# Attention units handled two at a time, with scores four units ahead and PSUM shared 4-2-2

## The chip, the core and the metric

The kernel runs on one core of one Trainium2 chip, as a single launch. The metric is the device time of that launch in microseconds (us). Five engines work side by side, each on its own stream of instructions in order: TensorE (PE; its weight loads have rows of their own, PEld), VectorE (DVE), ScalarE (ACT), GpSimd (POOL), and SyncE (SP), which here only issues DMAs. TensorE writes its results to PSUM, which holds eight banks of 128 partitions x 512 fp32; VectorE and ScalarE read them from there.

## The reference, cut to what matters

Attention with 32 global and 512 local positions per head (8 batches, 8 heads, head size 64), then a mixture of experts over all tokens:

```python
s_g = scale * q_g @ k_all.T            # global rows see everything
out_g = sm(s_g) @ v_all
s_ll = where(abs(i - j) <= 32, scale * q_l @ k_l.T, -1e9)   # a band of 32
s_l = concat([scale * q_l @ k_g.T, s_ll])                   # plus the global keys
out_l = sm(s_l) @ concat([v_g, v_l])
x = concat([out_g, out_l]) as (4352, 512)
logits = x @ w_gate                    # greedy: best (token, expert) pairs first, 544 tokens an expert
out[mask_e] = relu(x[mask_e] @ w1[e]) @ w2[e]
```

## The kernel before, in words

It has three stages in time: attention (with the gate's logits taken along), the routing, and eight experts. Only attention is touched by the change.

Attention works on **units**. A batch has ten: eight local units (`Local`, two heads by 256 rows each; two units share a pair of heads, that is one load of q, k and v) and two global units (`Glob`, four heads each). In the first seven batches the order is four local, one global, four local, one global; in the last it is two local, both global, six local. Each unit has four steps:

- `a`: scores on TensorE (L134; L195 for a global unit) into the PSUM tile `S`; a global unit takes two `S` tiles.
- `e`: mask, maximum and its negation on VectorE (L141, L143; L201 to L203), then the exponentials on ScalarE (L145; L210 to L216), into `p` (or `pg`).
- `c`: transposes of the exponentials on TensorE into the PSUM tile `T` (L150; L224, two tiles), and the copy `evac` from there into `pt` (or `pgt`).
- `d`: outputs on TensorE into the PSUM tile `O` (L162; L234), then the division on VectorE (L165 to L170; L237 to L241) into `xs` (or `xg`), which go to DRAM by DMA (L173, L243).

The gate's logits of a finished batch come as six extra steps, put between the units of the next batch: four `gate_x` (L259: transposes of one quarter of `xs` into `T`, copied by `evac` into `xt`; in the last batch into `S`), `gate_m` (L265: a product with the gate's weights into `O`, copied into `ltc`), and `gate_l` (L274: transposes into `T`, and a reduction on VectorE, L275, into `L`). The list `GS = (0, 2, 4, 6, 8, 9)` says in which units of the next batch they fall. The same steps for the global rows (`gx`) follow after the fourth and the eighth batch.

`evac` sends three of five copies to ScalarE (L251) and two to VectorE (L253). The order of the work is written out by hand: the loop below issues instructions, each engine runs its own in that order, and a tile with n buffers makes its n+1st writer wait for the first one's last reader. Every PSUM tile here is one bank: `S` 3, `T` 3, `O` 2.

```python
for i in range(-LA, nu + 3):              # LA = 2
    if i + LA < nu:
        ...                               # loads of later pairs
        units[i + LA].a()
    if 0 <= i < nu:
        units[i].c()
    if i + LA < nu:
        units[i + LA].e()
    if 1 <= i <= nu:
        units[i - 1].d()
    for f in extra.get(i, []):
        f()
```

`load_qk` brings q and k by DMA, and GpSimd spreads q into `qz` (L86); `load_v` brings v into `vw`. They are issued ahead, as the loop comes to a unit.

Of the kernel before, what the change touches and what calls it, by code (L numbers as in the profile page):

```python
# [8 lines left out]
F32 = mybir.dt.float32  # L9
# [9 lines left out]
B, H, SL, SG, D = 8, 8, 512, 32, 64  # L19
S = SL + SG  # L20
DM = H * D
# [4 lines left out]
NB = SL // 128  # L26
NW = SL // 32
# [37 lines left out]
def attention(ctx, tc, A, consts, xd, ident, L, nbatch, rt=None):  # L65
    nc = tc.nc
    ac = ctx.enter_context(tc.tile_pool(name="ac", bufs=1))
    ld = ctx.enter_context(tc.tile_pool(name="ld", bufs=3))
# [18 lines left out]
        return spread  # L87

    def load_v(b, p):
        t = ld.tile([128, 2, NW, D + 1], F32, name="vw", bufs=6)  # L90
        nc.sync.dma_start(t.rearrange("p h w d -> p (h w d)"), A["vw"][b, p])
        vw[b, p] = t

    qz = [ac.tile([128, QW // 32, 2, 32], F32, name=f"qz{i}") for i in range(NZ)]
    pg = [ac.tile([128, 6, 128], F32, name=f"pg{i}") for i in range(2)]
    mask = ac.tile([128, 2 * NB, 128], F32, name="mask")
    wg = ac.tile([128, 4, 32], F32, name="wg")
    P = [(b, p) for b in range(nbatch) for p in range(NP)]

    warm = ac.tile([128, 128], F32, name="warm")  # L100
    nc.vector.memset(warm, 0.0)
    wt = ps.tile([128, NB, 128], F32, name="T", bufs=3)
    for _ in range(WARM):
        nc.tensor.matmul(wt[:, 0, :], warm, warm, start=True, stop=True)
    for i in range(NZ):
        nc.gpsimd.memset(qz[i][64:128, :, 0, :], 0.0)
        nc.gpsimd.memset(qz[i][0:64, :, 1, :], 0.0)
    for i in range(2):
        nc.gpsimd.memset(pg[i], 0.0)
    load_qk(0, 0)(nc.vector)  # L110
    nc.sync.dma_start(mask.rearrange("p a b -> p (a b)"), A["mask"])
# [7 lines left out]
    class Local:  # L119
# [3 lines left out]
        def a(s):  # L123
            b, q = s.b, s.q
            z = qz[(b * NP + q) % NZ]
            kw = qk[b, q]
            st = ps.tile([128, NB, 128], F32, name="S", bufs=3)
            s.p = wk.tile([128, NB, 128], F32, name="p", bufs=4)
            s.nm = wk.tile([128, NB], F32, name="nm", bufs=4)
            for c in range(NB):  # L130
                for r in range(2):
                    j = 8 * s.u + 2 * c + r
                    k0 = 32 * ((3 * j + 1) // 2)
                    nc.tensor.matmul(st[64 * r:64 * r + 64, c, :], z[:, j].rearrange("p h i -> p (h i)"),  # L134
                                     kw[:, k0:k0 + 128], start=True, stop=True)
            s.st = st
# [8 lines left out]
                nc.scalar.activation(s.p[:, c, :], s.p[:, c, :], AF.Exp, bias=nm[:, c:c + 1], scale=SCALE)  # L145

        def c(s):
            t = ps.tile([128, NB, 128], F32, name="T", bufs=3)
            for c in range(NB):
                nc.tensor.transpose(t[:, c, :], s.p[:, c, :], ident)  # L150
            s.pt = wk.tile([128, NB, 128], F32, name="pt", bufs=3)
            evac(s.pt, t)
# [22 lines left out]
    class Glob:  # L175
# [2 lines left out]

        def a(s):
            b, g = s.b, s.g  # L180
            s.sa = ps.tile([128, 512], F32, name="S", bufs=3)
            s.sb = ps.tile([128, 32], F32, name="S", bufs=3)
            for part in range(2):
                for r in range(2):
                    i = 2 * g + r
                    t = qk[b, i]
                    z = qz[(b * NP + i) % NZ][:, NW].rearrange("p h i -> p (h i)")
                    if part == 0:
                        base = t[:, 64:128]
                        mv = ap_of(base, 0, [list(base.ap[0]), [96, 8], [1, 64]])  # L190
                        dd = s.sa[64 * r:64 * r + 64].rearrange("p (a b) -> p a b", b=64)
                    else:
                        mv = t[:, 32:64]
                        dd = s.sb[64 * r:64 * r + 64]
                    nc.tensor.matmul(dd, z, mv, start=True, stop=True)  # L195

        def e(s):
            b, g = s.b, s.g
            m = wk.tile([128, 8], F32, name="gm", bufs=2)
            s.m = m  # L200
            nc.vector.tensor_reduce(m[:, 0:1], s.sa, axis=AX.X, op=ALU.max)  # L201
            nc.vector.tensor_reduce(m[:, 1:2], s.sb, axis=AX.X, op=ALU.max)
            nc.vector.tensor_scalar(m[:, 2:3], m[:, 0:1], m[:, 1:2], -SCALE, op0=ALU.max, op1=ALU.mult)  # L203
            pgt = pg[(b * 2 + g) % 2]
            s.p = pgt
            f = pgt.rearrange("p a b -> p (a b)")
            d0 = f[:, 0:64]
            d1 = f[:, 512:576]
            pd = list(d0.ap[0])
            nc.scalar.activation(ap_of(d0, 0, [pd, [256, 2], [96, 3], [1, 64]]),  # L210
                                 s.sa[:, 0:384].rearrange("p (a b c) -> p a b c", a=2, c=64), AF.Exp,
                                 bias=m[:, 2:3], scale=SCALE, accum_out=m[:, 3:4])
            nc.scalar.activation(ap_of(d1, 0, [pd, [192, 2], [1, 64]]),
                                 s.sa[:, 384:512].rearrange("p (b c) -> p b c", c=64), AF.Exp,
                                 bias=m[:, 2:3], scale=SCALE, accum_out=m[:, 4:5])
            nc.scalar.activation(f[:, 672:704], s.sb, AF.Exp,  # L216
                                 bias=m[:, 2:3], scale=SCALE, accum_out=m[:, 5:6])

        def c(s):
            s.pt = wk.tile([128, 6, 128], F32, name="pgt", bufs=2)  # L220
            for lo, n in ((0, 4), (4, 2)):
                t = ps.tile([128, NB, 128], F32, name="T", bufs=3)
                for k in range(n):
                    nc.tensor.transpose(t[:, k, :], s.p[:, lo + k, :], ident)  # L224
                evac(s.pt[:, lo:lo + n], t[:, :n])
# [27 lines left out]
            nc.vector.tensor_copy(dst, src)  # L253

    def gate_x(src, xt, c, spare):
        t = ps.tile([128, NB, 128], F32, name="S" if spare else "T", bufs=3)
        n = src.shape[1]
        for k in range(n):
            nc.tensor.transpose(t[:, k, :], src[:, k, c * 128:(c + 1) * 128], ident)  # L259
        evac(xt[:, c, :n * 128], t[:, :n].rearrange("p a b -> p (a b)"))  # L260

    def gate_m(xt, n):
        lt = ps.tile([128, 512], F32, name="O", bufs=2)
        for c in range(4):
            nc.tensor.matmul(lt[32 * c:32 * c + 32, :n * 128], wg[:, c, :], xt[:, c, :n * 128],  # L265
                             start=True, stop=True)
        ltc = wk.tile([128, 512], F32, name="ltc", bufs=2)
        evac(ltc[:, :n * 128], lt[:, :n * 128])
        return ltc

    def gate_l(ltc, J, n):
        t = ps.tile([128, NB, 4, 32], F32, name="T", bufs=3)
        for k in range(n):
            nc.tensor.transpose(t[:, k].rearrange("p a b -> p (a b)"), ltc[:, k * 128:(k + 1) * 128], ident)  # L274
        nc.vector.tensor_reduce(L[:, J:J + n, :], t[:, :n, :, 0:8].rearrange("p k c e -> p k e c"),  # L275
                                axis=AX.X, op=ALU.add)

    def gate_units(b, src, J, n):
        xt = []

        def go(c):
            if c == 0:
                xt.append(wk.tile([128, 4, 128 * n], F32, name=f"xt{n}", bufs=2))
            if c < 4:
                gate_x(src(), xt[0], c, b == nbatch - 1)
            elif c == 4:
                xt.append(gate_m(xt[0], n))
            else:
                gate_l(xt[1], J, n)
        return [lambda c=c: go(c) for c in range(6)]  # L290
# [1 line left out]
    gsrc = {}  # L292

    def load_gx(i):
        t = wk.tile([128, 1, DM], F32, name="gx", bufs=2)
        for k in range(4):
            nc.sync.dma_start(t[32 * k:32 * k + 32, 0, :], xd[(4 * i + k) * S:(4 * i + k) * S + SG, :])
        gsrc[i] = t

    units = []  # L300
# [29 lines left out]
    def pairidx(u):  # L330
        if isinstance(u, Local):
            return u.b * NP + u.q
        return u.b * NP + 2 * u.g + 1

    nu = len(units)
    first = rt.setup(slice(0, 28)) if rt else None
    LA = 2
    for i in range(-LA, nu + 3):
        if rt and i == 2:
            rt.load()  # L340
        if rt and i == 12:
            rt.prepare()
        if i + LA < nu:
            while nl[0] < len(P) and nl[0] <= pairidx(units[i + LA]) + 4:
                load_qk(*P[nl[0]])(nc.gpsimd)
                load_v(*P[nl[0] - 1])
                nl[0] += 1
                if nl[0] == len(P):
                    load_v(*P[-1])
            units[i + LA].a()  # L350
        if 0 <= i < nu:
            units[i].c()
        if i + LA < nu:
            units[i + LA].e()
            if i + LA == 0:
                spread1(nc.vector)
        if 1 <= i <= nu:
            units[i - 1].d()
        for f in extra.get(i, []):
            f()  # L360
        if rt and i >= nu - 3:
            for _ in range(6):
                next(first, None)


WARM = 10
# [637 lines left out]
```

## Time and profile before

| what | value |
|---|---|
| median of 3 runs | 756.08 us (755.35 to 756.97) |
| the profiled execution | 756.55 us, span of its instructions 754.5 us |
| mean granted TensorE clock | 0.964 |
| PE busy | 697.2 us (92% of the span) |
| DVE busy | 504.8 us (67%) |
| ACT busy | 313.8 us (42%) |
| POOL busy | 159.7 us (21%) |
| data moved by DMA | 120.51 MB, mean 160 GB/s |

The profile's page gives the span in 40 slices of about 19 us, a digit for the busy tenths of each. A row of a window gives its bounds and length, then for PE, PEld, DVE, ACT and POOL the busy time and the number of instructions, then the granted clock, the DMA engines' busy share and GB/s. A row of the timeline gives the start, the length, the engine, the line, the operation, output tile<-input tiles, shapes, the count, and in brackets how long the engine was idle before it and what ended that. TensorE's own ends are modelled; the starts of its weight loads show best when a group could begin.

### The profile page before, as it was taken

The page shows a single profiled execution, that of the slowest core. Times are in us where ns is not written, and L with a number is a line of the kernel's source. Part 1 is how long each engine was busy: PE and PEld are TensorE (multiplying, and loading weights), DVE is VectorE, ACT ScalarE, POOL GpSimd, SP SyncE. Part 2 cuts the span into 40 slices and gives each one's busy share as a digit, 9 for nine tenths or more (in the row PEclk, how much of TensorE's full clock was granted, in tenths as well). Part 3 has the DMA queues.
Part 4 walks back from the last instruction along what each step waited for, and adds up shares of the span by engine and source line. Part 5 has one row for each costly group of instructions (what it writes and reads, how often), then busy time and mean ns, then how long its engine had stood idle before and what let it go on. Part 6 is the DMA issues. An engine that isn't in the chain of part 4 may idle for free. (4 is left out here: it accounts for less than half of the span.)

```text
span 754.5 us, 21122 instructions
## 1 busy us (share of the span) xinstructions
PE 697.2 (92%) x8636; PEld 560.2 (74%) x8636; DVE 504.8 (67%) x1848; ACT 313.8 (42%) x849; POOL 159.7 (21%) x190
## 2 busy tenths in 40 slices
PE   7989999999995189999999999999999999899993
PEld 6767777777673179768779878877877878888972
DVE  5887878877777778767767777766776774441300
ACT  3656665665651034234143244234333333443310
POOL 5222112221100130241241241141132043312011
PEclk9999999999998569999999999999999999999997
DMA  9997879969701160360161161261072065231000
GB/s 359 405 364 286 323 280 332 338 244 333 289 22 58 45 238 1 111 204 29 70 234 40 62 240 43 71 212 62 8 260 78 1 254 186 75 126 46 1 33 28
DMA packets 32416, 120.51 MB, mean 160 GB/s; under 512 B 6720, under 2 KB 6976, under 8 KB 24128
## 3 DMA queue, kind: packets, MB, share of 16 engines
q1 hardware_dynamic: 22080, 67.78, 24.1%
q0 software_dynamic: 10240, 51.39, 19.4%
q8 instruction: 68, 1.11, 0.6%
q14 instruction: 28, 0.23, 0.1%
HBM read 101.32 MB, written 17.83 MB: 158 GB/s over the span
## 5 line engine op out<-in xcount | busy, mean ns | idle before, releaser
L860 PE MATMUL H<-xh,w1h 128*128 128x272 f32 x512 | 153.0, 299 | 3.6 <-DVE hl L405 3.0
L860 PE MATMUL H<-xl,w1h 128*128 128x272 f32 x512 | 151.4, 296 | 0.0
L860 PE MATMUL H<-xh,w1l 128*128 128x272 f32 x512 | 151.4, 296 | 0.0
L145 ACT ACTIVATE p<-p,nm 128x128 f32<-128x128 f32 x256 | 82.1, 394 | 65.1 <-DVE ls L165 33.1
L862 ACT ACTIVATE hh<-H 128x272 fp32r<-128x272 f32 x128 | 51.0, 399 | 135.3 <-PE H L860 129.8
L888 PE MATMUL Y<-w2h,hh 128*128 128x512 f32 x256 | 103.9, 406 | 0.0
L860 PEld LDWEIGHTS H<-xh,w1h 128*128 128x128 f32 x512 | 98.0, 191 | 7.0 <-DVE hl L405 2.7
L888 PE MATMUL Y<-w2l,hh 128*128 128x512 f32 x256 | 102.8, 401 | 0.0
L888 PE MATMUL Y<-w2h,hl 128*128 128x512 f32 x256 | 102.4, 400 | 0.0
L860 PEld LDWEIGHTS H<-xl,w1h 128*128 128x128 f32 x512 | 97.9, 191 | 0.6
L860 PEld LDWEIGHTS H<-xh,w1l 128*128 128x128 f32 x512 | 97.8, 191 | 0.3
L134 PE MATMUL S<-qk,qz 128*64 128x128 f32 x1024 | 71.2, 281 | 5.5 <-DVE qz L86 2.9
L405 DVE SCALAR_TENSOR_TENSOR hl<-H,hh 128x272 fp32r<-128x272 f32 x128 | 54.6, 435 | 26.5 <-ACT h L864 12.6
L86 POOL COPY qz<-q 64x544 f32<-64x544 f32 x60 | 38.3, 639 | 149.6 <-DMA q<-in_qk_dram 109.6
L134 PEld LDWEIGHTS S<-qk,qz 128*64 128x64 f32 x1024 | 55.5, 138 | 18.3 <-issue 11.0
L742 POOL DMA_INDIRECT out_dram<-y,idx x40 | 39.7, 992 | 137.9 <-ACT y L833 84.7
L405 DVE TENSOR_TENSOR w2l<-w2r,w2h 128x512 fp32r<-128x512 f32 x64 | 43.2, 688 | 37.6 <-ACT w2h L712 37.2
L696 POOL DMA_INDIRECT w1r<-in_w_dram,widx x16 | 15.7, 979 | 229.8 <-DVE r_a L405 127.2
L141 DVE CUSTOM_DVE_ANT_0 p<-S,mask 128x128 f32<-128x128 f32 x256 | 58.7, 286 | 6.1 <-PE S L134 5.6
L833 ACT ACTIVATE y<-Y 128x512 f32<-128x512 f32 (+1 forms) x40 | 23.2, 595 | 92.8 <-PE Y L888 59.4
L888 PEld LDWEIGHTS Y<-w2h,hh 128*128 128x128 f32 x256 | 48.2, 188 | 15.8 <-issue 5.9
L712 ACT ACTIVATE w1h<-w1r 128x512 fp32r<-128x512 f32 x64 | 36.5, 624 | 49.7 <-DVE L L405 29.8
(168 smaller groups left out, 1200.7 us busy)
## 6 DMA issues: line engine op xcount, KB each, us to landing
vw<-in_vw_dram SPq DMA_DIRECT2D x32, 1040.0 KB, 7.8
qk<-in_qk_dram SPq DMA_DIRECT2D x32, 432.0 KB, 5.4
q<-in_qk_dram SPq DMA_DIRECT2D x32, 272.0 KB, 5.8
xd<-xs SPq DMA_DIRECT2D x8, 1024.0 KB, 6.8
xd<-xg SPq DMA_DIRECT2D x64, 8.0 KB, 5.3
xg<-xd,idx POOLq DMA_INDIRECT x40
out_dram<-y,idx POOLq DMA_INDIRECT x40
mask<-in_mask_dram SPq DMA_DIRECT2D x1, 512.0 KB, 4.5
```

What stands on the lines that cost most here:

```text
L86: eng.tensor_copy(z[r, :, h, :], q[r].rearrange("p (j i) -> p j i", i=32))
L134: nc.tensor.matmul(st[64 * r:64 * r + 64, c, :], z[:, j].rearrange("p h i -> p (h i)"), kw[:, k0:k0 + 128], start=True, stop=True)
L141: nc.vector.tensor_tensor_reduce(s.p[:, c, :], st[:, c, :], mask[:, 4 * s.u + c, :], 1.0, -BIG, ALU.add, ALU.max, nm[:, c:c + 1])
L145: nc.scalar.activation(s.p[:, c, :], s.p[:, c, :], AF.Exp, bias=nm[:, c:c + 1], scale=SCALE)
L405: return op(*args, **kw)
L696: nc.gpsimd.indirect_dma_start(out=dst, out_offset=None, in_=src, element_offset=off, in_offset=bass.IndirectOffsetOnAxis(ap=idx, axis=0))
L712: nc.scalar.activation(hi, raw, AF.Copy)
L742: nc.gpsimd.indirect_dma_start(out=out, out_offset=bass.IndirectOffsetOnAxis(ap=rt.idx[ph][:n, t:t + 1], axis=0), in_=y[:n], in_offset=None)
L833: nc.scalar.activation(y[:n], p[:n], AF.Copy)
L860: nc.tensor.matmul(p, w[d][:, fs], x[:, d, q], start=(d + k == 0), stop=(d + k == 5))
L862: nc.scalar.activation(hh[:, f, q], p, AF.Relu)
L888: nc.tensor.matmul(p, h[:, f, q], w[f], start=(f + k == 0), stop=(f + k == 9))
```

## The change

Attention's loop takes two units per pass. In each pass come the transposes and copies (`c`) of both, the scores (`a`) of two units four ahead, their reductions and exponentials (`e`), the outputs (`d`) of the two units just transposed, and then the extra steps of two units. `LA` goes from 2 to 4. PSUM is shared anew: `S` 4, `T` 2, `O` 2. Work buffers grow (`p`, `nm`, `gm`, `pg`, `vw`) and others shrink to one (`ltc`, `xt`, `gx`). The loads move behind `c`.

```diff
-    pg = [ac.tile([128, 6, 128], F32, name=f"pg{i}") for i in range(2)]
+    pg = [ac.tile([128, 6, 128], F32, name=f"pg{i}") for i in range(3)]
...
-            st = ps.tile([128, NB, 128], F32, name="S", bufs=3)
-            s.p = wk.tile([128, NB, 128], F32, name="p", bufs=4)
-            s.nm = wk.tile([128, NB], F32, name="nm", bufs=4)
+            st = ps.tile([128, NB, 128], F32, name="S", bufs=4)
+            s.p = wk.tile([128, NB, 128], F32, name="p", bufs=6)
+            s.nm = wk.tile([128, NB], F32, name="nm", bufs=8)
...
-            t = ps.tile([128, NB, 128], F32, name="T", bufs=3)
+            t = ps.tile([128, NB, 128], F32, name="T", bufs=2)
...
-        t = ps.tile([128, NB, 128], F32, name="S" if spare else "T", bufs=3)
+        t = ps.tile([128, NB, 128], F32, name="S" if spare else "T", bufs=4 if spare else 2)
...
-        ltc = wk.tile([128, 512], F32, name="ltc", bufs=2)
+        ltc = wk.tile([128, 512], F32, name="ltc", bufs=1)
...
-                xt.append(wk.tile([128, 4, 128 * n], F32, name=f"xt{n}", bufs=2))
+                xt.append(wk.tile([128, 4, 128 * n], F32, name=f"xt{n}", bufs=1))
...
-    LA = 2
-    for i in range(-LA, nu + 3):
+    LA = 4
+    for i in range(-LA, nu + 2, 2):
+        now = (i, i + 1)
...
+        for k in now:
+            if 0 <= k < nu:
+                units[k].c()
+        for k in now:
+            if k + LA < nu:
+                ...
+                units[k + LA].a()
+        for k in now:
+            if k + LA < nu:
+                units[k + LA].e()
...
+        for k in now:
+            if 0 <= k < nu:
+                units[k].d()
+        for k in now:
+            for f in extra.get(k + 1, []):
+                f()
```

The vw tile goes from 6 to 7 buffers, gm from 2 to 4, gx from 2 to 1.

More of the change, by code (lines that the diff above doesn't have):

```diff
@@ L89, in load_v @@
     def load_v(b, p):
-        t = ld.tile([128, 2, NW, D + 1], F32, name="vw", bufs=6)
+        t = ld.tile([128, 2, NW, D + 1], F32, name="vw", bufs=7)
         nc.sync.dma_start(t.rearrange("p h w d -> p (h w d)"), A["vw"][b, p])
@@ L101, in attention @@
     nc.vector.memset(warm, 0.0)
-    wt = ps.tile([128, NB, 128], F32, name="T", bufs=3)
+    wt = ps.tile([128, NB, 128], F32, name="T", bufs=2)
     for _ in range(WARM):
@@ L107, in attention @@
         nc.gpsimd.memset(qz[i][0:64, :, 1, :], 0.0)
-    for i in range(2):
+    for i in range(3):
         nc.gpsimd.memset(pg[i], 0.0)
@@ L180, in a @@
             b, g = s.b, s.g
-            s.sa = ps.tile([128, 512], F32, name="S", bufs=3)
-            s.sb = ps.tile([128, 32], F32, name="S", bufs=3)
+            s.sa = ps.tile([128, 512], F32, name="S", bufs=4)
+            s.sb = ps.tile([128, 32], F32, name="S", bufs=4)
             for part in range(2):
@@ L198, in e @@
             b, g = s.b, s.g
-            m = wk.tile([128, 8], F32, name="gm", bufs=2)
+            m = wk.tile([128, 8], F32, name="gm", bufs=4)
             s.m = m
@@ L203, in e @@
             nc.vector.tensor_scalar(m[:, 2:3], m[:, 0:1], m[:, 1:2], -SCALE, op0=ALU.max, op1=ALU.mult)
-            pgt = pg[(b * 2 + g) % 2]
+            pgt = pg[(b * 2 + g) % 3]
             s.p = pgt
@@ L221, in c @@
             for lo, n in ((0, 4), (4, 2)):
-                t = ps.tile([128, NB, 128], F32, name="T", bufs=3)
+                t = ps.tile([128, NB, 128], F32, name="T", bufs=2)
                 for k in range(n):
@@ L271, in gate_l @@
     def gate_l(ltc, J, n):
-        t = ps.tile([128, NB, 4, 32], F32, name="T", bufs=3)
+        t = ps.tile([128, NB, 4, 32], F32, name="T", bufs=2)
         for k in range(n):
@@ L294, in load_gx @@
     def load_gx(i):
-        t = wk.tile([128, 1, DM], F32, name="gx", bufs=2)
+        t = wk.tile([128, 1, DM], F32, name="gx", bufs=1)
         for k in range(4):
@@ L342, in attention @@
             rt.prepare()
[L343 to L363, printed above, removed]
+        for k in now:
[3 more added lines that the diff above has]
+            if k + LA < nu:
+                while nl[0] < len(P) and nl[0] <= pairidx(units[k + LA]) + 4:
+                    load_qk(*P[nl[0]])(nc.gpsimd)
+                    load_v(*P[nl[0] - 1])
+                    nl[0] += 1
+                    if nl[0] == len(P):
+                        load_v(*P[-1])
+                units[k + LA].a()
+        for k in now:
+            if k + LA < nu:
+                units[k + LA].e()
+                if k + LA == 0:
+                    spread1(nc.vector)
+        for k in now:
[4 more added lines that the diff above has]
+                f()
+            if rt and k >= nu - 4:
+                for _ in range(6):
+                    next(first, None)
 WARM = 10
```

## The prediction

> **What bounds the kernel now.** I read the page first, for where TensorE is busy and at what clock, then the table of windows over the attention stage, then the timeline of TensorE's weight loads, which shows every idle piece between groups.
>
> ```profile
> PE   7989999999995189999999999999999999899993
> PEclk9999999999998569999999999999999999999997
> ```
> ```profile
> 98.19:125.37 27.18, 27.13 (x569) 20.18 (x568) 22.35 (x128) 17.78 (x56) 5.11 (x8) 1.00 0.84 306
> 125.37:152.44 27.07, 27.07 (x571) 20.19 (x570) 21.51 (x118) 17.99 (x57) 5.11 (x8) 1.00 0.88 320
> 202.51:236.41 33.90, 31.53 (x625) 22.30 (x621) 24.89 (x120) 17.73 (x55) 0.00 (x0) 1.00 0.22 76
> ```
> ```profile
> 98.19 0.20 PEld L195 LDWEIGHTS S<-qk,qz 128*64 128x64 f32 x4 [0.17 <-issue]
> ...
> 100.47 0.85 PEld L134 LDWEIGHTS S<-qk,qz 128*64 128x64 f32 x16
> 101.49 0.42 PEld L150 LDWEIGHTS T<-ident,p 128*128 128x128 f32 x4 [0.17 <-issue]
> 102.08 0.50 PEld L162 LDWEIGHTS O<-vw,pt 128*32 128x32 f32 x32 [0.17 <-issue]
> 102.67 0.42 PEld L259 LDWEIGHTS T<-ident,xs 128*128 128x128 f32 x4
> 103.26 0.85 PEld L134 LDWEIGHTS S<-qk,qz 128*64 128x64 f32 x16 [0.17 <-issue]
> ...
> 125.37 0.20 PEld L195 LDWEIGHTS S<-qk,qz 128*64 128x64 f32 x4 [0.17 <-issue]
> ...
> 152.44 0.20 PEld L195 LDWEIGHTS S<-qk,qz 128*64 128x64 f32 x4 [0.17 <-issue]
> ```
>
> The page's slices 13 to 15 are the routing between attention (to 236.41 us) and the experts. The change touches attention alone, so all of its effect must come from the first 236 us. From slice 5 on, attention keeps TensorE at 9 tenths or more. The first score group of a batch's first global unit recurs every 27.18 and 27.07 us, and the windows cut there show TensorE busy 27.13 of 27.18 and 27.07 of 27.07 us. VectorE is busy for 22 us, ScalarE for 18, the DMA engines for 0.84 to 0.88. TensorE bounds the stage; nothing makes it wait today.
>
> The weight loads show what it spends. A local unit costs a score group (100.47 to 101.49: 1.02), a transpose group (0.59) and an output group (0.59): 2.20 us. A gate transpose takes another 0.59. Each slot ends in a piece of about 0.17 in which nothing is loaded, wherever the next group has another shape (128*64, 128*128, 128*32).
>
> **The change, step by step.** First what it saves.
>
> ```profile
> 225.44 0.42 PEld L259 LDWEIGHTS S<-ident,xs 128*128 128x128 f32 x4
> 225.83 0.47 PEld L150 LDWEIGHTS T<-ident,p 128*128 128x128 f32 x4
> ...
> 226.47 0.50 PEld L162 LDWEIGHTS O<-vw,pt 128*32 128x32 f32 x32 [0.17 <-ACT p L145]
> ```
> ```profile
> 90.94 0.50 PEld L162 LDWEIGHTS O<-vw,pt 128*32 128x32 f32 x32 [0.17 <-issue]
> 91.37 0.19 PEld L265 LDWEIGHTS O<-xt,wg 128*32 128x32 f32 x8
> 92.39 0.85 PEld L134 LDWEIGHTS S<-qk,qz 128*64 128x64 f32 x16 [0.84 <-issue]
> ```
>
> Two transpose groups in a row took 1.03 (225.44 to 226.47), not 1.18; an output group followed by the gate's matmul, of the same shape, gave up its slot after 0.43, not 0.59. So a change of shape costs 0.16. Per batch there are now 35 of them: three for each of ten units, one for each of four gate transposes (they sit between outputs and scores), one for the gate's last step. Afterwards there are 15: three for each of five pairs, for a gate transpose now stands ahead of the next pair's transposes. Twenty fewer are 3.2 us a batch, 23.9 instead of 27.1, if TensorE waits for nothing.
>
> [...]
>
> Now what it adds. Transposes have two PSUM banks (T) instead of three. In a pair's pass the order on every engine is: c, c (transposes and their copies out), a, a (scores), e, e (reductions, exponentials), d, d (outputs), gates. A gate transpose takes the bank of the first c; of the next pair the first c takes the other bank, and the second needs the gate's bank back. That bank is freed by the gate's copy, which in program order stands behind both e's exponentials on ScalarE, or behind e, e, d, d on VectorE. Behind the waiting transpose on TensorE stand the next scores, and e waits for these: the loop closes, and its length is the period of a pair. Today the same late copy is harmless, because a third bank is at hand:
>
> ```profile
> 140.34 0.66 PE L259 MATMUL T<-ident,xs 128*128 128x128 f32 x4
> ...
> 142.25 0.60 ACT L251 ACTIVATE xt<-T 128x512 f32<-128x512 f32 x1
> ```
>
> The gate transposed at 140.34 was copied out at 142.25 only, after the exponentials issued ahead of it. The rows that price the loop:
>
> ```profile
> 149.42 1.09 PE L134 MATMUL S<-qk,qz 128*64 128x128 f32 x16
> ...
> 150.56 0.29 DVE L141 CUSTOM_DVE_ANT_0 p<-S,mask 128x128 f32<-128x128 f32 x1 [0.58 <-PE S L134]
> ```
> ```profile
> 9.94 0.29 DVE L141 CUSTOM_DVE_ANT_0 p<-S,mask 128x128 f32<-128x128 f32 x1
> ...
> 10.91 0.17 DVE L143 TENSOR_SCALAR nm<-nm 128x4 f32<-128x4 f32 x1
> ...
> 11.11 1.29 ACT L145 ACTIVATE p<-p,nm 128x128 f32<-128x128 f32 x4 [0.65 <-DVE nm L143]
> 11.14 0.29 DVE L141 CUSTOM_DVE_ANT_0 p<-S,mask 128x128 f32<-128x128 f32 x1
> ```
> ```profile
> 101.06 0.15 DVE L165 TENSOR_SCALAR ls<-O 128x4 f32<-128x4 f32 x1
> ...
> 101.80 0.28 DVE L141 CUSTOM_DVE_ANT_0 p<-S,mask 128x128 f32<-128x128 f32 x1
> ```
> ```profile
> 146.95 1.29 ACT L145 ACTIVATE p<-p,nm 128x128 f32<-128x128 f32 x4 [2.32 <-DVE nm L143]
> 148.15 0.58 ACT L251 ACTIVATE ltc<-O 128x512 f32<-128x512 f32 x1
> ```
> ```profile
> 227.64 0.58 ACT L251 ACTIVATE pt<-T 128x512 f32<-128x512 f32 x1
> ...
> 228.28 0.50 PEld L162 LDWEIGHTS O<-vw,pt 128*32 128x32 f32 x32 [0.80 <-ACT pt L251]
> ...
> 230.00 0.68 DVE L253 COPY pt<-T 128x512 f32<-128x512 f32 x1
> ...
> 230.73 0.50 PEld L162 LDWEIGHTS O<-vw,pt 128*32 128x32 f32 x32 [0.40 <-DVE pt L253]
> ```
>
> Count from the start of a pair's first scores. The first reduction starts at 1.14 (149.42 to 150.56: it waits for the whole unit's scores). One e occupies VectorE for 1.20 (9.94 to 11.14), so the second starts at 2.34 and its maximum is ready 1.14 later (9.94 to 10.91 + 0.17), at 3.48. Its exponentials start 0.03 later, and the next ScalarE instruction 1.20 after that (146.95 to 148.15), at 4.71. A copy on ScalarE ends at 5.29, the transpose starts 0.06 later (228.22 to 228.28), at 5.35, and 0.59 after that come the next scores: 5.94. On VectorE the two d's follow at 3.54, 0.74 each (101.06 to 101.80), to 5.02; the copy of 0.68 ends at 5.70, the transpose starts at 5.75 (230.68 to 230.73), the scores at 6.34. Three copies of five go to ScalarE, so the mean is 6.10. Today two units with one gate transpose take 2 x 2.20 + 0.59 = 4.99. TensorE alone would reach the second transposes at 3.72 (1.70 of scores, 0.84 of outputs, 0.42 each for the gate and the first c, two changes of 0.17), so it waits 1.6 to 2.0 us.
>
> A batch's five pairs, with a global unit's e and d taken as equal to a local's. The pairs with the 1st and 3rd gate transposes: 6.10 each. After the 2nd the next pair holds a global unit first, whose transposes need two banks, so that the local's also wait for the global's first copy (0.58 to 0.68 behind the gate's when on the same engine): 6.55. After the 4th a global unit comes second, and its last group waits for the local's copy: 6.38. The fifth pair now has the gate's matmul and its last step back to back:
>
> ```profile
> 150.45 0.66 PE L150 MATMUL T<-ident,p 128*128 128x128 f32 x4
> ...
> 151.20 0.60 ACT L251 ACTIVATE pt<-T 128x512 f32<-128x512 f32 x1 [0.82 <-PE T L150]
> ...
> 224.56 0.28 DVE L275 TENSOR_REDUCE L<-T 128x32 f32<-128x128 f32 x1
> ```
>
> The gate's matmul needs an output bank, of which there are two and both are in use: it waits for the first d on VectorE, to 4.28. It runs 1.02 (91.37 to 92.39), its result is seen 0.16 after that (as a transpose's: 0.75 at 151.20 against its slot of 0.59), its copy takes 0.58 to 0.68, and the last step's transposes start at 6.19. Their reduction (0.75 later, 0.28 long) frees the bank for the second c at 7.27; next scores 7.86. Together 6.10 + 6.55 + 6.10 + 6.38 + 7.86 = 33.0, which is 5.9 above 27.1. Six batches (2nd to 7th) carry such gates: +35.4.
>
> The rest. The last batch, now 33.90: its first two pairs carry two gate transposes each (about 7.7 and 6.7 by the same rows), then there are no more scores between c and d, so each d waits for its copy; I get some 32.7, -1.2, with ends -3 and +4. The first batch has no gates and could use the fewer changes (up to -3.2), but needs its loads two units sooner while TensorE still waits for them in the page's first three slices, and one more score group runs ahead of the first transposes (+1): 0 taken, ends -3 and +3. The third pg fill on GpSimd, the larger work buffers and the loads moved behind c lie beside DMA waits and cost nothing: GpSimd is busy 5.11 of 27 us. The single xt, ltc and gx buffers are written a pass or more after their last read. A longer stage asks less of the DMA engines than 0.88.
>
> Sum: 35.4 - 1.2 + 0 = +34. The profiled execution took 756.55 (median of the runs 756.08); 756.55 + 34 gives 790. The banks' wait isn't seen in the trace of before; its low end is 0 (the first rival), its high end the loop above. I take the loop, because each of its links is a row and none can be passed on an engine that works in order. If a reduction needed only its own quarter of the scores, the loop would be 0.6 shorter: 30 passes, 18 us, 772.
>
> **Rivals.** (1) The wait is hidden and only the saving is left: 756.55 - 8 x 3.2 = 731. It decides at one point: the gate's copy must end by 3.7 after the scores' start, not 5.3. VectorE, at 21.5 to 22.4 us a batch, leaves room for 23.9. Against it: the copy at 142.25, which stood in line. (2) The banks come back in time, but the matmul and last step of the gate do not: four pairs at 4.7 (VectorE's own work, two e's, two d's and a copy or so) and one at 7.8 give 26.6 a batch, about 752. It needs the same early copy. (3) The clock falls in the waits:
>
> ```profile
> 9.98 0.88 PEld L134 LDWEIGHTS S<-qk,qz 128*64 128x64 f32 x16 [3.13 <-POOL pg L109]
> ...
> 11.98 1.57 PEld L134 LDWEIGHTS S<-qk,qz 128*64 128x64 f32 x16 [0.33 <-PE T L150]
> ```
>
> After 3.13 us of idling a score group was loaded over 1.57, not 0.85. If every pass ran so, its scores and transposes would take about 1.1 more: 30 passes, +33, 823. Against it: the waits here stay under 2 us, and the window from 202.51 held 1.00 with 2.4 us of idle time in pieces. [...]
>
> **How the numbers follow.** The loop of two banks: 0.80, at 790, of its own 765 to 810. Rival 1: 0.11. Rival 2: 0.04. Rival 3: 0.05. About 0.2% is what a measurement of this kernel can tell from no change. Rivals 1 and 2 are faster; with 0.01 for a cancellation this gives faster 0.15, same 0.01, slower 0.84. The range 765 to 810 leaves out the rivals.
>
> **What would show it.** In the changed kernel's timeline the weight loads come in runs of 32 for scores and 64 for outputs; the first global scores recur every 33 us; transposes (L150) wait 1.6 to 2.0 us for the copy of xt, four times a batch; the gate's matmul waits for VectorE's xs and its last step for ltc; TensorE falls to about 75% in a batch and the DMA share to about 0.7. The prediction is wrong if the period is 24 to 25 us, if the gate's copy starts ahead of the second e's exponentials, or if the granted clock drops below 1.00 between 60 and 220 us.

## The result: 796.1 us, 5.3% slower than before

| | before | after |
|---|---|---|
| median | 755.97 us (755.35 to 756.97, 4 runs) | 796.1 us (794.32 to 798.01, 4 runs) |
| after / before | | 1.0525 [1.0499, 1.0552] |
| profiled execution (span) | 756.55 us (754.5) | 798.01 us (796.0) |
| mean granted TensorE clock | 0.964 | 0.957 |
| attention's last transposes start at | 235.82 us | 279.24 us |
| from there to the end of the span | 518.7 us | 516.8 us |

The forecast was 790 (765 to 810). The whole loss lies in attention: it ends 43.4 us later, and the routing and the experts give 1.9 us back. The page of after shows it in the first 14 slices:

```profile
PE   7868878777777724999999999999999999999993
```

Attention now takes 14 slices, in which TensorE is busy for 6 to 8 tenths. The windows of after cut the stage into the first ten units (from the first global scores on), the next sixty, and the rest; a clean batch stands below, and the sixty units of before below that:

```profile
15.20:44.10 28.90, 22.32 (x533) 18.30 (x532) 19.53 (x113) 16.89 (x55) 7.64 (x12) 0.94 0.99 396
44.10:243.86 199.76, 157.10 (x3407) 121.92 (x3406) 134.77 (x716) 105.68 (x331) 29.25 (x46) 0.98 0.71 250
243.86:279.82 35.96, 28.38 (x564) 21.36 (x562) 22.63 (x109) 15.24 (x41) 0.00 (x0) 0.95 0.17 56
```
```profile
113.42:145.53 32.11, 25.47 (x569) 20.08 (x568) 22.33 (x119) 16.72 (x53) 5.09 (x8) 0.99 0.74 260
```
```profile
36.00:202.51 166.51, 162.82 (x3411) 120.58 (x3410) 133.24 (x727) 104.54 (x329) 31.96 (x50) 1.00 0.85 313
```

TensorE is busy for a little less in the sixty units (157.1 against 162.8 us), but they take 199.76 us instead of 166.51: +33.3. The first ten units add 8.1 (the eleventh unit's transposes start at 44.10 instead of 36.00), the last ten and the final gate steps 2.1 (35.96 against 33.90); unrounded, 8.10 + 33.25 + 2.06 make the 43.4.

The timeline of TensorE's weight loads over that clean batch shows what it waits for:

```profile
118.90 0.42 PEld L150 LDWEIGHTS T<-ident,p 128*128 128x128 f32 x4 [1.34 <-ACT pt L251]
119.48 1.73 PEld L134 LDWEIGHTS S<-qk,qz 128*64 128x64 f32 x32 [0.17 <-issue]
121.38 0.95 PEld L162 LDWEIGHTS O<-vw,pt 128*32 128x32 f32 x64 [0.17 <-issue]
122.43 0.42 PEld L259 LDWEIGHTS T<-ident,xs 128*128 128x128 f32 x4
122.81 0.47 PEld L224 LDWEIGHTS T<-ident,pg 128*128 128x128 f32 x4
124.78 0.20 PEld L224 LDWEIGHTS T<-ident,pg 128*128 128x128 f32 x2 [1.50 <-ACT xt L251]
124.95 0.47 PEld L150 LDWEIGHTS T<-ident,p 128*128 128x128 f32 x4
...
131.11 0.42 PEld L150 LDWEIGHTS T<-ident,p 128*128 128x128 f32 x4 [1.43 <-ACT xt L251]
131.69 1.73 PEld L134 LDWEIGHTS S<-qk,qz 128*64 128x64 f32 x32 [0.17 <-issue]
...
136.99 0.64 PEld L224 LDWEIGHTS T<-ident,pg 128*128 128x128 f32 x6 [1.49 <-ACT pt L251]
137.79 1.73 PEld L134 LDWEIGHTS S<-qk,qz 128*64 128x64 f32 x32 [0.17 <-issue]
...
142.01 0.19 PEld L265 LDWEIGHTS O<-xt,wg 128*32 128x32 f32 x8 [1.15 <-PE O L234]
143.91 0.42 PEld L274 LDWEIGHTS T<-ident,ltc 128*128 128x128 f32 x4 [1.71 <-DVE ltc L253]
```

The runs of 32 scores and 64 outputs are there, and so is the loop: the gate's four transposes (122.43) go at once, the first of the next unit's (122.81) too, and the next group stands until the gate's copy has left the other bank. In the last pair the gate's product and its last step wait in turn; the product started at 142.01, after VectorE had read the first output (141.47 + 0.42), and the PE group that its row names had ended before.

Two of the four rows (118.90 and 136.99) name the copy of `pt`, not of `xt`. There the gate's copy fell to VectorE and ended at 118.98 and 137.09, after TensorE had gone on; ScalarE's copy of the pair's own first unit ended at 118.85 and 136.94. So the waiting group took whichever of the two banks came free first, and not strictly the next in turn; this is read from the times, for the profile doesn't name the bank. Most of the waits are for `xt`, all the same. From 40 to 205 us, the two largest sums of TensorE's waits for another engine are these (us in all, times, longest):

```profile
PEld T L224 <- ACT xt L251: 8.1, 6, 1.6
PEld T L150 <- ACT xt L251: 7.2, 7, 1.4
```

From the second batch's first global scores to the seventh's (45.13 to 212.78), weight loads waited 24.3 us for copies of `xt` (18 times), 7.1 for `pt` or `pgt` and 8.4 for `ltc`. In before, that stretch has 0.5 us of such waits. It grew by 28.8 us, less than the waits, for there are also fewer changes of shape (0.16 us each, by the rows of before).

On VectorE and ScalarE, in the pass whose scores start at 119.48:

```profile
120.63 0.29 DVE L141 CUSTOM_DVE_ANT_0 p<-S,mask 128x128 f32<-128x128 f32 x1 [1.65 <-PE S L134]
...
122.63 0.17 DVE L143 TENSOR_SCALAR nm<-nm 128x4 f32<-128x4 f32 x1
```
```profile
121.80 2.45 ACT L145 ACTIVATE p<-p,nm 128x128 f32<-128x128 f32 x8 [1.55 <-DVE nm L143]
124.16 0.57 ACT L251 ACTIVATE xt<-T 128x512 f32<-128x512 f32 x1
```

The gate's transposes had been loaded by 122.85 (122.43 + 0.42), but ScalarE first finishes eight exponentials, and its copy starts at 124.16. VectorE had waited 1.65 us for the scores, which TensorE could not start before 119.48.

### The profile page after: what moved, and what is told of

Same layout as the page of the kernel before. It is cut to its first block, busy times and chain, and to the rows that moved or that the text cites. A ratio compares the mean times of both kernels' runs of the same rounds, so it can differ in the third digit from the quotient of the medians.

```text
span 796.0 us, 21078 instructions
## 1 busy us (share of the span) xinstructions
PE 688.4 (86%) x8636; PEld 562.5 (71%) x8636; DVE 506.8 (64%) x1848; ACT 314.9 (40%) x849; POOL 159.5 (20%) x191
## 5 line engine op out<-in xcount | busy, mean ns | idle before, releaser
L145 ACT ACTIVATE p<-p,nm 128x128 f32<-128x128 f32 x256 | 79.5, 390 | 71.7 <-DVE nm L143 63.5
L134 PE MATMUL S<-qk,qz 128*64 128x128 f32 x1024 | 66.6, 282 | 3.5 <-DVE qz L86 3.5
L894 PEld LDWEIGHTS Y<-w2h,hl 128*128 128x128 f32 x256 | 48.2, 188 | 10.1 <-issue 0.2
```

The costliest lines, as they stand in the source:

```text
L894: nc.tensor.matmul(p, h[:, f, q], w[f], start=(f + k == 0), stop=(f + k == 9))
```

## The experiments

Each ratio is to the kernel before, run beside it on the same chip. "End" is the start of attention's last transposes in the profiled execution; "five batches" is the time from the second batch's first global scores to the seventh's.

| kernel | us / before | ratio | end | five batches |
|---|---|---|---|---|
| before | | | 235.82 | 138.85 |
| after | 796.1 / 755.97 | 1.0525 [1.0499, 1.0552] | 279.24 | 167.65 |
| e1 gate in S | 772.87 / 752.22 | 1.0255 [1.0210, 1.0299] | 264.18 | 159.92 |
| e2 PSUM 3-3-2 | 773.64 / 752.22 | 1.0281 [1.0236, 1.0326] | 258.83 | 154.78 |
| e3 gates before e | 791.05 / 752.22 | 1.0515 [1.0467, 1.0563] | 276.07 | 167.97 |
| e5 gates after c, 3-3-2 | 773.58 / 757.47 | 1.0215 [1.0187, 1.0243] | 252.55 | 149.77 |
| e6 before, gates after c | 753.41 / 757.47 | 0.9945 [0.9923, 0.9967] | 235.73 | 138.01 |
| e7 before, PSUM 4-2-2 | 758.85 / 752.22 | 1.0069 [1.0043, 1.0096] | 247.02 | 147.17 |
| e8 pairs for locals only | 751.93 / 755.67 | 0.9948 [0.9928, 0.9968] | 233.47 | 138.82 |
| e9 e8, v loaded once | 744.36 / 755.12 | 0.9848 [0.9767, 0.9928] | 228.71 | 132.94 |
| e10 before, v loaded once | 751.92 / 755.12 | 0.9947 [0.9917, 0.9977] | 234.21 | 137.99 |
| e11 after, v loaded once | 792.80 / 755.12 | 1.0486 [1.0403, 1.0568] | 275.11 | 166.15 |

What follows attention took between 510.3 and 518.7 us in these profiles. Part of what attention gains or loses is so given back or added later; why was not tested, and the parts of the loss are therefore read from "end" and the timelines.

**e1, the gate's transposes out of T.** One line of `gate_x`, in the changed kernel:

```diff
-        t = ps.tile(..., name="S" if spare else "T", bufs=4 if spare else 2)
+        t = ps.tile(..., name="S", bufs=4)
```

> The changed kernel, but the gate's transposes (gate_x) always take an S bank instead of a T bank. Bank theory (the second transposes of a pair wait for the bank of the gate's copy): the four waits a batch that follow a gate_x and precede two local units vanish, pairs 1 and 3 of a batch fall from 6.1 to about 4.7 us; pairs next to a global unit stay near 5.8, since a global and a local unit need three T banks by themselves; the pair with gate_m and gate_l stays at 7.7. Period about 28.9 instead of 32.1 us, time about 775. Rival (the order of a pair's pass, with VectorE's work, sets the period and the bank doesn't matter): 32.1 and 796 stay. Clock theory (the falls of the clock make the excess): a few us less, 790.

Measured: 772.87. The ratio, 1.0255, is what 775 beside the 755.97 of the result would have given; attention ends 15.1 us earlier than in after. The period was missed: the five batches took 32.0 us each, not 28.9. The granted clock averaged 0.95 over them (0.98 in after), and some stops and waits were longer than in the rows below, up to 2.60 in mid-group and 4.0 for `pgt`. That the time came out is so partly luck; what this run shows is the pair of locals. The timeline of weight loads:

```profile
112.47 0.95 PEld L162 LDWEIGHTS O<-vw,pt 128*32 128x32 f32 x64 [0.17 <-issue]
113.52 0.42 PEld L259 LDWEIGHTS S<-ident,xs 128*128 128x128 f32 x4
113.91 0.91 PEld L150 LDWEIGHTS T<-ident,p 128*128 128x128 f32 x8
...
116.88 0.95 PEld L162 LDWEIGHTS O<-vw,pt 128*32 128x32 f32 x64 [0.17 <-issue]
...
120.42 0.42 PEld L150 LDWEIGHTS T<-ident,p 128*128 128x128 f32 x4 [1.43 <-DVE pgt L253]
```

A pair of locals with a gate transpose now recurs after 4.41 (112.47 to 116.88) instead of 6.1, though the gate's copy still stands behind the exponentials: only its bank is another. So the T bank that the gate holds is what stopped a pair of locals. The next rows show what is left: a global and a local unit together need three T banks without any gate, and the third waits 1.43.

**e2, a third T bank.** The changed kernel's order with `S` 3, `T` 3, `O` 2.

> The changed kernel with PSUM shared 3-3-2 as before (S 3, T 3, O 2) and the order of the pairs unchanged. Bank theory: waits after a gate_x vanish, a local unit's transposes after a global's still wait when a gate_x stands ahead of them (four banks needed): period about 28.4 us; in the first batch the wait of 2.67 us at 25.5 us goes too; time about 770. Rival (order alone): 796. If three S banks are too few for four units ahead: scores (L134, L195) wait for VectorE or ScalarE, and the period is above 32.

Measured: 773.64, a ratio of 1.0281, where 770 beside the before of the result (755.97) would be 1.0186: about 7 us above the expectation. The five batches took 31.0 us each, not 28.4. The end moves by 20.4 against after. In the first batch, which carries no gates, the local unit after a global one goes at once (22.82; after had waited 2.67 there, shown below), and the eleventh unit's transposes start at 40.30, not 44.10:

```profile
22.82 0.47 PEld L150 LDWEIGHTS T<-ident,p 128*128 128x128 f32 x4
```

**e3, the extra steps between the scores and the reductions.** In the changed kernel the loop over `extra` moves from behind `d` to behind `a`, for the first seventy units.

> The changed kernel with banks 4-2-2 as they are, but the extra steps moved from the end of the pass to between a and e, except in the last batch, so that their copies stand ahead of the exponentials and reductions on their engines. Bank theory: the gate's bank comes back in time; pairs 1 and 3 fall to 4.7 us, pairs beside a global unit stay near 5.9, the gate_m and gate_l pair falls to about 6.5 because gate_m finds its output bank free: period about 27.8, time about 770. Rival (too few banks whatever the order): 796.

Measured: 791.05; the expectation failed by 21 us, by the ratio by 25. What it said of local pairs held; what it left out is in the second and third rows:

```profile
113.22 1.81 PEld L134 LDWEIGHTS S<-qk,qz 128*64 128x64 f32 x32 [0.17 <-issue]
116.04 0.42 PEld L259 LDWEIGHTS T<-ident,xs 128*128 128x128 f32 x4 [1.01 <-ACT pt L251]
...
119.74 0.42 PEld L150 LDWEIGHTS T<-ident,p 128*128 128x128 f32 x4 [1.42 <-DVE pgt L253]
```

The pair before 113.22 took 4.66 (from 108.56), so with its copy ahead of the exponentials a gate costs little. But the gate's transposes, now put right behind the pair's own, themselves wait for the copy of `pt` (1.01), and pairs with a global unit keep their wait (1.42; a second one in that batch, at 132.50, took 2.95). With two banks for up to four tiles a pass, moving the gate only moves the wait.

**e5, gates right behind `c`, with three T banks.** The changed kernel with 3-3-2, `gate_x` and `gate_l` behind `c`, and `GS = (0, 2, 4, 6, 7, 8)`.

> Pairs with PSUM shared 3-3-2, the gate's transposes right behind a pair's own (so their copies stand ahead of e, and they need no change of shape), gate_m behind the outputs of the fourth pair and gate_l behind the transposes of the fifth. Bank theory with the saving of the prediction (0.16 us for each change of shape that goes): no wait for a gate's copy, VectorE sets about 4.7 us a pair, period about 24.5 instead of 27.1 us, some 15 us below the kernel before. Rival (loads or instructions can't follow: the DMA share rises to 0.95 and TensorE stops inside groups, as it did at 35.6 and 43.5 us): no more than 5 us below it. Rival (order alone makes pairs slow): 15 us or more above it.

Measured: 773.58, 16 us slower than before, where some 15 faster was expected: a clear miss. One pair of locals did take 4.51 (132.09 to 136.60). A pair with a global unit and a gate has four T tiles for three banks, and took 6.20 (136.60 to 142.80):

```profile
139.54 0.64 PEld L224 LDWEIGHTS T<-ident,pg 128*128 128x128 f32 x6
140.14 0.47 PEld L150 LDWEIGHTS T<-ident,p 128*128 128x128 f32 x4
142.21 0.42 PEld L259 LDWEIGHTS T<-ident,xs 128*128 128x128 f32 x4 [1.60 <-ACT pgt L251]
```

I had counted banks for local pairs only. That made the rule for e8: no pass may hold more T tiles than there are banks.

**e6, one unit at a time, gates behind `c`.** In the kernel before, the extra steps move from the end of the pass to behind `c` (except in the last ten units), so that a gate's transposes follow transposes.

> The kernel before, one unit per pass and 3-3-2, with the gate's steps moved from the end of the pass to behind c. The price of a change of shape tested by itself: a gate_x behind a unit's transposes needs one change fewer, as does gate_l, 5 a batch at 0.16 us, seven batches: 5 us below the kernel before (0.7%). If the pieces of 0.17 us were not lost time: within 0.2%. If copies collide: above it.

Measured: 753.41, a ratio of 0.9945, 4.1 us below before, close to the 5 expected. The trace gives it only part of the support. A batch without a long stop took 26.19 us, where before took 27.07 (125.37 to 152.44):

```profile
125.00:151.19 26.19, 26.19 (x576) 20.39 (x569) 21.09 (x113) 17.83 (x56) 5.11 (x8) 1.00 0.95 321
```

Five changes of shape fewer, at 0.16, make 0.80 of these 0.88. But the five batches gained only 0.8 together, other stops taking the rest, and the profiled attention ended where it did before (235.73). The price of a change of shape is shown in that batch; that the whole 0.55% comes from it is not.

**e7, the bank share alone.** The kernel before with `S` 4, `T` 2, `O` 2.

> The kernel before with PSUM shared 4-2-2 and nothing else changed: one unit per pass, two units ahead. Bank theory: little is lost, since there a copy has only one unit's e ahead of it and the next use of its bank is two groups away: 756 to 765. Rival (two T banks are too few in any order): the waits for copies of xt show here too, +20 us or more.

Measured: 758.85, 0.7% slower, inside the expectation. Taken one unit at a time, two T banks nearly suffice: a clean batch took 26.88 us (105.72 to 132.60; before 27.07), and over the five batches TensorE waited 3.6 us for copies out of T, where after waited 31.4 for the same three (`xt`, `pt`, `pgt`). Attention still ended 11.2 us later than in before, more than the time shows; in two of the batches the clock was down (0.97 and 0.92), and one stop in mid-group took 2.75. It is the pair's pass that makes two banks too few: the banks alone cost 0.7%, the order alone (e2) 2.8%, and both together 5.3%; by attention's end, 11.2, 23.0 and 43.4 us. Either way the whole is more than the sum.

**e8, pairs for local units only.** Global units get a pass of their own, `gate_x` and `gate_l` use `S` banks behind `c`, and `gate_m` stands between `a` and `e`; scores run two passes ahead; PSUM stays 4-2-2. The core of the edit:

```diff
-            us = loc[:4] + [gl[0]] + loc[4:] + [gl[1]]
+            groups += [loc[:2], loc[2:4], gl[:1], loc[4:6], loc[6:], gl[1:]]
```

> Banks 4-2-2 and pairs for local units, but a global unit has a pass of its own (so that no pass needs three T banks), scores two passes ahead; the gate's transposes, gate_l's too, stand right behind c and use S banks; gate_m stands between a and e, gate_l two or more passes later. If the waits for banks (a gate's copy, a global unit's second bank, gate_m's output bank) are the whole loss of the change: no pass waits for a copy, four pairs at 4.7 us and two single passes at about 2.8 make a period of 25.5 instead of 27.1 us, and the time is 5 to 10 us below the kernel before. If pairs lose by something else too (clock, instruction or load supply in the first 60 us): the period in the middle is still 25.5, but the first ten units take longer than the 25 us of before, and the time is within 4 us of it. If in-order copies still stand behind exponentials in a single pass: waits of 1 us or more at outputs (L162, L234) for pt or pgt, and no gain.

Measured: 751.93, ratio 0.9948, 3.7 us below before and 44 below after (1.0525 - 0.9948 of 756); a little less than expected. It is faster than both kernels. Attention ends at 233.47, 45.8 us earlier than in after. It changes several things at once, so it shows their sum: pairs need not lose once the banks suffice. It keeps the rest of the change (the work buffers, the loads behind `c`), so that can't be what costs after its time. The period was missed: 27.8 us a batch, as in before, not 25.5. Outputs waited for `pt` (4.9 us in the five batches, up to 1.7), as the third case of the expectation had it, and more was lost in waits for no engine:

```profile
109.69 0.85 PEld L162 LDWEIGHTS O<-vw,pt 128*32 128x32 f32 x52
112.96 0.26 PEld L162 LDWEIGHTS O<-vw,pt 128*32 128x32 f32 x12 [2.42 <-issue]
```

A group of 64 output loads stops for 2.42 us after the 52nd. The next three kernels ask why.

**e9, e10, e11, the load traffic.** The kernels e8, before and after, each with `load_v` cut short:

```diff
     def load_v(b, p):
+        if b * NP + p >= 7:                 # 6 in e10
+            vw[b, p] = vw[divmod((b * NP + p) % 7, NP)]
+            return
```

> Pairs for the local units, global units alone, gates in S banks (the kernel of e8), with v loaded for the first seven pairs of heads only; later units use these tiles again, so the output isn't the reference's. In e8 TensorE stands still in the middle of groups, waiting for nothing that the profile shows: 2.42 us at 112.96, 1.88 at 132.78, 1.96 at 38.14. Theory (the stops are the supply of TensorE's instructions, late when the DMA queues are full): with the v traffic gone after the seventh pair the DMA share falls, the stops after about 55 us shrink below 1 us, and the kernel takes 5 to 9 us less than e8's ratio gives, about 0.985 of the kernel before on the same chip. Rival (the stops belong to TensorE or to the order of the work): they stay, in the same places, and the ratio stays at 0.995.

> The kernel before, with v loaded for the first six pairs of heads only; later units use these tiles again, so the output isn't the reference's. Control for the theory of instruction supply: the kernel before has stops in the middle of groups of 1.28 us at 38.36 and 1.50 at 45.81 only, and 0.56 at 70.52. By the theory those after 45 us go and the kernel takes 1 to 3 us less (ratio 0.996 to 0.999). By the rival nothing moves (1.000). If the loads themselves held units up, it would gain more than 3 us.

> The changed kernel with v loaded for the first seven pairs of heads only; later units use these tiles again, so the output isn't the reference's. Theory (the loop of the two T banks sets the period of a pair): with less DMA traffic nothing changes from the second batch on, the pairs still recur every 6.1 us and the batch every 32 to 33, and the ratio to the kernel before stays at 1.045 to 1.053; only stops in mid-group, about 3 us in the first batch, can go. Rival (the loss is DMA or instruction supply): the batch falls below 30 us and the ratio below 1.03.

Measured: e9 0.9848, as the theory of supply said; of the 7.6 us that it gains on e8's ratio, attention's end shows 4.8. The same output group, and the window from 60 to 160 us, first of e8 and then of e9:

```profile
60.00:160.00 100.00, 91.26 (x2085) 74.75 (x2081) 78.23 (x434) 61.90 (x196) 17.92 (x28) 1.00 0.86 305
```
```profile
60.00:160.00 100.00, 95.96 (x2227) 79.99 (x2217) 83.83 (x466) 66.16 (x212) 20.48 (x32) 1.00 0.54 166
```
```profile
110.47 0.98 PEld L165 LDWEIGHTS O<-vw,pt 128*32 128x32 f32 x64 [0.56 <-ACT pt L254]
```

With the DMA share down from 0.86 to 0.54, e9 loads 7% more weights in the same time (2217 against 2081), the group of 64 comes unbroken, and the longest unexplained stop in mid-group after 60 us is 0.43 instead of 2.42. In the first 60 us, before the traffic is gone, one of 1.96 stays, as in e8. e10 has none above 0.4 in mid-group after 60 us either, but gained 3.2 us or so in the whole, a little more than expected, of which its attention's end shows 1.6; the rest lies behind attention, whose data are others in these three kernels.

e11 is the control for the prediction. A clean batch of it:

```profile
109.47:141.12 31.65, 25.23 (x569) 19.99 (x568) 22.09 (x119) 16.87 (x54) 5.09 (x8) 1.00 0.40 129
```
```profile
114.71 0.42 PEld L153 LDWEIGHTS T<-ident,p 128*128 128x128 f32 x4 [1.34 <-ACT pt L254]
...
120.59 0.20 PEld L227 LDWEIGHTS T<-ident,pg 128*128 128x128 f32 x2 [1.50 <-ACT xt L254]
...
139.50 0.42 PEld L277 LDWEIGHTS T<-ident,ltc 128*128 128x128 f32 x4 [1.71 <-DVE ltc L256]
```

At nearly half the DMA share (0.40 against 0.74) the batch takes 31.65 instead of 32.11, and the waits are the same 1.34, 1.50 and 1.71. The ratio, 1.0486, overlaps after's. So what costs the changed kernel its time from the second batch on is the loop of the banks, not DMA or the supply of instructions.

## Why the prediction was right, step by step

**The loop.** Its links, counted from the pair's first scores at 119.48:

| link | forecast | measured |
|---|---|---|
| first reduction starts | 1.14 | 1.15 (120.63) |
| second maximum ready | 3.48 | 3.32 (122.63 + 0.17) |
| gate's copy starts | 4.71 | 4.68 (124.16) |
| waiting transposes start | 5.35 | 5.30 (124.78) |
| next scores | 5.94 | 6.10 (125.58; six transposes ahead of them here, not four) |

It closes as forecast, though two of the agreements are partly luck. The copy's start had two chains of equal length in the forecast, over the second unit's maximum and over ScalarE's eight exponentials. VectorE's `e` took 1.05 instead of 1.20 (120.63 to 121.68), so that the maximum came early, and the other chain set the start: 2.32 after the scores' start (121.80) and 2.36 of exponentials. And the mean period of 6.10 was made of 5.94 and 6.34. No pair took the way of 6.34: where the gate's copy fell to VectorE, TensorE went on with the bank that ScalarE's copy of `pt` had freed, and those pairs took 6.06 and 6.10.

TensorE waited 1.34 to 1.50 us four times a batch, a little under the 1.6 to 2.0, because it came to the waiting group a bit later than the 3.72 I had counted: at 123.28, 3.80 after the scores' start (122.81 + 0.47). e1 and e3 show both halves of the reason: another bank, or a copy ahead of the exponentials, brings a pair of locals down to 4.4 to 4.9.

**The batch.** The scores of the five pairs start at 113.42, 119.48, 125.58, 131.69 and 137.79, the next batch's at 145.53: 6.06, 6.10, 6.11, 6.10 and 7.74, against 6.10, 6.55, 6.10, 6.38 and 7.86. The two larger ones were mis-sized. I let the local unit wait for the global's first copy behind the gate's on one engine; the copies went to two (`xt` on ScalarE, `pgt` on VectorE, three and two of five in turn), and at 124.95 the local's transposes followed at once. In the fourth pair, too, the two copies ran side by side (`xt` on VectorE at 136.41, `pt` on ScalarE at 136.37), and the global's six transposes went together at 136.99. So a clean batch takes 32.11, not 33.0. The sixty units took 199.76, where six times 33.0 is 198. That the loss was 33.3 and not 35.4 is due to the other side: I took before's 27.1 of two clean batches for all six, and its sixty units took 166.51, which is 27.75 each. In after, other batches were longer than the clean one: the stretch from the sixth batch's first global scores to the seventh's (177.41 to 212.78, 35.37) also holds the gate steps of the global rows, which I had not charged for the T banks, and the one from 79.90 to 113.42 took 33.52 in a window whose clock was down, in part:

```profile
60.00:113.42 53.42, 42.75 (x915) 33.21 (x911) 35.19 (x190) 28.14 (x86) 8.90 (x14) 0.95 0.65 229
```

**The first ten units: forecast 0, measured +8.1, outside its own bounds of -3 and +3.** This step failed. I looked for loads and for the extra score group, not for the banks, since there are no gates yet. After's timelines of TensorE and of ScalarE:

```profile
22.21 0.64 PEld L224 LDWEIGHTS T<-ident,pg 128*128 128x128 f32 x6
25.52 0.72 PEld L150 LDWEIGHTS T<-ident,p 128*128 128x128 f32 x4 [2.67 <-ACT pgt L251]
26.56 1.58 PEld L134 LDWEIGHTS S<-qk,qz 128*64 128x64 f32 x16 [0.33 <-issue]
...
33.70 0.59 PEld L162 LDWEIGHTS O<-vw,pt 128*32 128x32 f32 x34 [0.17 <-issue]
35.62 0.49 PEld L162 LDWEIGHTS O<-vw,pt 128*32 128x32 f32 x30 [1.33 <-issue]
...
43.53 0.48 PEld L234 LDWEIGHTS O<-vw,pgt 128*32 128x32 f32 x26 [2.89 <-issue]
44.10 0.86 PEld L150 LDWEIGHTS T<-ident,p 128*128 128x128 f32 x8
```
```profile
22.54 2.45 ACT L145 ACTIVATE p<-p,nm 128x128 f32<-128x128 f32 x8 [2.49 <-DVE nm L143]
24.89 0.84 ACT L251 ACTIVATE pgt<-T 128x512 f32<-128x512 f32 x2
```

A global unit takes two T tiles and the local behind it a third: the loop in small, with the copy of `pgt` again behind eight exponentials. It costs 2.67 and then the clock (loads of 0.72 and 1.58 instead of 0.42 and 0.85). Two stops in mid-group add 1.33 and 2.89. e2, where the local goes at once, brings back 3.8 of the 8.1; its stops are shorter by 1.7 together, and it has a new wait of 2.26 (33.46). e11, whose stops are 1.61 and 1.52 there and whose clock stayed up behind the same wait (2.52), brings back 2.5. How the 8.1 divides is thus known only roughly.

**The last ten: forecast -1.2, measured +2.1,** inside the bounds of -3 and +4. The clock averaged 0.95 there, where before held 1.00: 1.00 up to 272 us and 0.78 from there on, behind a wait of 2.18 for `pt` (272.92). Two waits for the gate's copy, which I had priced in, came to 1.50 and 1.42 (250.39, 258.21); the parts were not tested by themselves. **Behind attention** I had counted nothing; it gave 1.9 back.

The sum, 35.4 - 1.2 + 0, was 34; measured, 33.3 + 2.1 + 8.1 - 1.9 is about 41.5, the difference of the spans. The mechanism carried the sign and four fifths of the size, and the step that failed is the first batch.

**The rivals.** The first (731, the wait is hidden) and the second (752, only the last pair pays) both needed the gate's copy to end by 3.7; it ended at 5.25 (124.16 + 0.57). The third, the falling clock, held in places only: 0.98 over the sixty units, not half speed in every pass. My own sign for it, a clock below 1.00 between 60 and 220 us, was met, so that part of the forecast was wrong in words. Its price is small: the missing 0.02 of 199.76 us is about 4 us, by estimate. I had also read the row for this rival too simply: the group right behind the 3.13 us (9.98) was loaded in 0.88, at full speed, and the one over 1.57 came 2 us later. DMA share at 0.71 and TensorE at 79% busy (157.10 of 199.76) came out near the 0.7 and 75%.

## What to carry to other kernels

Count, for each pass of a hand-ordered loop, the tiles that want a PSUM bank before the copy that frees it can run, and the place of that copy in its engine's queue; here a pass that wanted one bank more than there was had the way round that queue as its period (6.06 to 6.11 us), while TensorE was busy for only 79% of the sixty units. Grouping work to save changes of shape is worth some 0.16 us each here, and a single bank wait of 1.4 us undoes almost nine of them. When a loop has been freed of its waits, look at stops that wait for nothing: here they ended 1.25 to 1.63 us after a packet of an instruction queue, and the longest after 60 us fell from 2.42 to 0.43 us when the DMA share fell from 0.86 to 0.54.

## What the runs showed of the hardware

**TensorE's stops in mid-group end behind packets of an instruction queue.** In after, the stops in mid-group at 35.62 and 43.53 lie 126 weight loads apart (30 + 4 + 4 + 2 + 32 + 32 + 22, counted in the timeline), with as many matmuls, so about 252 instructions. The page lists a queue for instructions (packets, MB, share):

```profile
q8 instruction: 68, 1.11, 0.6%
```

That is 16.3 KB a packet. The same page counts 8636 matmuls and 8636 weight loads; if the 68 packets brought these and nothing else, each held 254 instructions, by estimate, and the spacing of 252 agrees with it. The traces also keep the time of every packet. In after, one ran from 33.10 to 34.19 and one from 41.13 to 42.14, and the two stops ended 1.43 and 1.39 us after them; in e8 one ran from 110.71 to 111.66, and the stop of 2.42 ended 1.30 after it. All 58 stops of 0.6 us or more in the middle of a group, in attention of the twelve kernels, end 1.25 to 1.63 us after such a packet has, though the packets come some 6 us apart. That TensorE stands there for want of the packet's instructions is read from these times; the profile names no releaser.

That the stops go with the load traffic is shown by e8 and e9 (2.42 and 0.43 us at a DMA share of 0.86 and 0.54). A busy stretch is not the whole condition: the longest stop of all, 3.53 us in e3 at 152.53, came at a share of 1.00 (145.0 to 152.5), but one of 2.60 in e1 at 104.16 at a share of 0.50 (99.0 to 104.2). A packet itself takes about 1 us in e8 and e9 alike (0.95 from 110.71, 0.88 from 112.68); what makes it start late, no run shows.

**A wait of 2.1 to 2.7 us was followed by a lower clock of TensorE, or not.** After 2.67 us of waiting in after, the loads at 25.52 and 26.56 took 0.72 and 1.58 us instead of 0.42 and 0.85, at a granted clock of 0.54 (25.5 to 28.9 us). In e11 the same wait, 2.52 there, left them at 0.42 and 0.85, and waits of 1.3 to 1.7 in after's clean batch left the clock at 0.99. In e1 it fell about a wait of 2.14 (four loads over 0.72), right behind a stop of 2.60 (104.16):

```profile
106.68 0.72 PEld L274 LDWEIGHTS T<-ident,ltc 128*128 128x128 f32 x4 [2.14 <-ACT ltc L251]
```

In e2 a wait of 2.26 left it up (33.46, the 32 scores behind it still took 1.73). So no limit for a single wait can be read from these runs: 2.14 us went with a fall, 2.52 without one. What else counted, no run here tells.
